# Pads of 448 and 64 bytes around the two weight tiles of one product

## The chip, the core and the metric

One core of a Trainium2 chip runs the whole program in one launch. The metric is device time in microseconds. The engines that matter are TensorE (PE; its weight loads are listed apart as PEld), VectorE (DVE), ScalarE (ACT), GpSimd (POOL) and the queue of SyncE (SP), which issues nearly all transfers.

## What is computed

Linear attention with random features, then a mixing of tokens by a low-rank matrix, then an MLP with a residual, all in float32:

```python
def phi(x):
    proj = np.einsum('bhsd,md->bhsm', x, omega)
    sq = np.sum(x * x, axis=-1, keepdims=True) / 2.0
    h = proj - sq
    h = h - np.max(h, axis=-1, keepdims=True)
    return np.exp(h) / np.sqrt(m)
kv = np.einsum('bhsm,bhsd->bhmd', k_p, v)
num = np.einsum('bhsm,bhmd->bhsd', q_p, kv)
den = np.einsum('bhsm,bhm->bhs', q_p, z)[..., None] + 1e-06
# x = num / den, heads joined: (8, 576, 512)
h = xt @ U @ V
u = x + h.transpose(0, 2, 1)
ch = np.maximum(u @ w_ch1, 0.0) @ w_ch2        # 512 -> 2048 -> 512
return (u + ch).astype(np.float32)
```

## The kernel before

The 8 x 576 = 4608 rows go through three phases. The first (to about 325 us) does the attention and the mixing; its projections, L766 to L768, multiply a feature matrix (`omh`, `oml`, the moving operand) with transposed queries and keys (`xh`, `xl`, the stationary operand). Each result u goes to DRAM.

The second phase is the MLP's first layer. Rows are taken in 9 chunks of 512, the 2048 hidden units in 4 groups of 512, and each product of a chunk with a group is done by Strassen's scheme: 7 products of halves, numbered 0 to 6. Every operand is split into a high and a low part of type float32r, so a product is 2 (f) x 2 (k) x 3 (high by high, low by high, high by low) = 12 matmuls of 128x128 by 256 columns (L1007). There the weight slice `wh` or `wl` is the stationary operand, and u (`uh`, `ul`) is the moving one. The results g go through the ReLU to DRAM.

The third phase is the second layer: 36 steps (chunk, half j, half s), again 7 products each, 12 matmuls a product (L1390). Here g (`gh`, `gl`) is stationary and the weights move. Step n has s = n mod 2, and k = 0 to 3 uses weight group (4 s + k) // 2, so that group 0 serves k = 0 and 1 of the 18 steps with s = 0.

Weights live in slots, one pair (`wh`, `wl`) for each group g and product i, got by `w_slot(g, i)`; a tile is 128 x 512 float32, 2048 bytes of each partition. Groups 0 and 1 lie in the pool `wa` at the bottom of the left stack, in the order in which they are first asked for; groups 2 and 3 lie in `wb` on the right stack. A slot serves the first layer, and later, by `w_place(g)`, the second layer's weights of the same group. Chunk 0 reads u from the pool `up` like the others, but chunk 1's u operands (`guest`) are put into slots of group 3 (`place=lambda i: w_slot(NG - 1, i + 2)`), and appear as `wh`, `wl` on both sides of L1007. Chunks 0 and 1 run first, in the order (0,0), (0,1), (1,0), (1,1), (0,2), (1,2) of (chunk, group); at group 3 their products alternate; after that come chunks 2 to 8, four groups each.

What lies where is set by stacks of pools and by pads: `shifted(stack, by)` opens a pool with one tile of `by` bytes that no instruction uses. Above `wa` on the left stack come `dec` (tiles of 2048 and 4096 bytes), then, in the first layer, a pad of 704 bytes and `up` (tiles of 2048 bytes, u among them). In the second layer `dec` and `up` are closed, and a pad of 320 bytes and the pool `vp` with the g operands stand straight above `wa`. So, modulo 512 bytes, u lies 704 and g 320 behind the weights. In the kernel as allocated every weight slot, left or right, begins 448 bytes past a multiple of 512.

All orders on the engines that touch the change are written out by hand (`K` keeps an instruction in program order).

Of the kernel before, what the change touches and what calls it, by code (L numbers as in the profile page):

```python
# [9 lines left out]
F32 = mybir.dt.float32  # L10
F32R = mybir.dt.float32r
# [18 lines left out]
def performer_mlp_kernel(ctx: ExitStack, tc, q, k, v, omega, U, V, w1, w2, out):  # L30
# [12 lines left out]
    P = 128  # L43
# [36 lines left out]
    wpools = {g: wa for g in range(EARLY_GROUPS)}  # L80
# [145 lines left out]

    def w_slot(g, i):
        i = (i - 2) % 7 if g == NG - 1 else i
        return [wpools[g].tile([P, 2, 2 * P], F32R, name=f"w{a}{g}_{i}") for a in "hl"]

    def operand(g, i):
        if (g, i) not in wops:
            if g == NG - 1 and i < 2:
                if not spares:
                    room = late["rx"].tile([P, 2, PIECE, 2], U32, name="graw0").bitcast(F32R)
                    spares.extend(room.rearrange("p s (k t) w -> p (s k) (t w)", k=2)[:, j] for j in range(4))
                wops[g, i] = [x.rearrange("p (k t) -> p k t", k=2) for x in spares[2 * i : 2 * i + 2]]
            else:
                wops[g, i] = w_slot(g, i)
        return wops[g, i]  # L240
# [826 lines left out]
    def w_place(g):  # L1067
        return lambda i: w_slot(g, i)
# [5 lines left out]
    tp = aside.enter_context(tc.tile_pool(name="tp", bufs=1))  # L1074
    guest_raws = loads(1, tp)
    guest = prepare(1, next(guest_raws), place=lambda i: w_slot(NG - 1, i + 2), lows=(VE, G_) * 3 + (VE,), pool=tp)
    for n, _ in enumerate(mixers[0]):
        if n == 2:
# [166 lines left out]
    for n in range(2, len(order)):  # L1245
        c, g = order[n]
# [123 lines left out]
    for n in range(NS):  # L1370
# [9 lines left out]
        for i in range(PRODUCTS):  # L1380
# [4 lines left out]
            for k in range(4):  # L1385
                g, f = divmod(now.s * 4 + k, 2)
# [70 lines left out]
```

## Time and profile before

| | us |
|---|---|
| median of 3 runs | 1037.36 |
| lowest and highest run | 1030.91, 1040.03 |
| the profiled execution | 1036.24 |
| its span | 1034.3 |
| TensorE busy | 1007.6 (97%) |
| VectorE busy | 850.4 (82%) |
| ScalarE busy | 613.7 (59%) |
| GpSimd busy | 519.8 (50%) |

The span is the time from the first to the last instruction of the profile. Matmuls are pipelined: a duration in the profile (276 ns, for example) is longer than the distance between the starts of two neighbours, and the next begins while the last is still under way. Where nothing waits, it is the distance between starts that adds up to the time.

### The profile page before, as it was taken

The page shows a single profiled execution, that of the slowest core. Times are in us where ns is not written, and L with a number is a line of the kernel's source. Part 1 is how long each engine was busy: PE and PEld are TensorE (multiplying, and loading weights), DVE is VectorE, ACT ScalarE, POOL GpSimd, SP SyncE. Part 2 cuts the span into 40 slices and gives each one's busy share as a digit, 9 for nine tenths or more (in the row PEclk, how much of TensorE's full clock was granted, in tenths as well). Part 3 has the DMA queues.
Part 4 walks back from the last instruction along what each step waited for, and adds up shares of the span by engine and source line. Part 5 has one row for each costly group of instructions (what it writes and reads, how often), then busy time and mean ns, then how long its engine had stood idle before and what let it go on. Part 6 is the DMA issues. An engine that isn't in the chain of part 4 may idle for free.

```text
span 1034.3 us, 23873 instructions
## 1 busy us (share of the span) xinstructions
PE 1007.6 (97%) x8497; PEld 985.9 (95%) x8497; DVE 850.4 (82%) x1502; ACT 613.7 (59%) x1483; POOL 519.8 (50%) x457
## 2 busy tenths in 40 slices
PE   8999899999998989999999999999999999999998
PEld 7899899999996989999999999999999999999998
DVE  4798898898898787766567465779999999999995
ACT  5889789989885555545355353764535444444442
POOL 3446766967534544233415214445664645646643
PEclk9899899999999999999999999999999999999999
DMA  7687578587444775987678678874545545455451
GB/s 138 137 167 147 114 176 171 107 184 154 87 103 96 210 183 137 248 246 196 186 202 215 187 183 255 254 234 135 211 147 177 181 166 175 150 184 174 142 175 51
DMA packets 380630, 175.51 MB, mean 170 GB/s; under 512 B 275680, under 2 KB 353504, under 8 KB 376032
## 3 DMA queue, kind: packets, MB, share of 16 engines
q1 hardware_dynamic: 378144, 173.70, 63.4%
q8 instruction: 67, 1.10, 0.4%
q10 hardware_dynamic: 2368, 0.30, 0.2%
q14 instruction: 51, 0.42, 0.1%
HBM read 109.97 MB, written 63.96 MB: 168 GB/s over the span
## 4 chain that ended last, share of the span: by engine, by line
PE 56%; DVE 3%; DMA 3%; issue 2%; ACT 1%; POOL 1%; SPq 0%; ACTq 0%; DVEq 0%; POOLq 0%
PE p_p L1390 9%; PE p_q L1390 8%; PE p_n L1390 7%; PE p_n L1007 7%; PE p_p L1007 5%; PE p_q L1007 5%; PE p_kv L1390 4%; PE p_kv L1007 4%; PE p_m L1007 4%; PE p_m L1390 2%; DVE g L995 1%; DMA g<-g 1%; DMA graw<-in_moe_w_ch_dram 1%; DMA graw<-g 0%; DVE wl L537 0%
## 5 line engine op out<-in xcount | busy, mean ns | idle before, releaser
L781 ACT ACTIVATE e<-p_p,nm 128x128 f32<-128x128 f32 x576 | 166.2, 397 | 27.9 <-DVE nm L774 22.3
L1228 ACT CAST gh<-gs 128x512 fp32r<-128x512 f32 x140 | 86.4, 622 | 153.4 <-DVE gs L1200 90.3
L1200 POOL TENSOR_TENSOR gs<-graw 128x512 f32<-128x512 f32 x70 | 111.2, 1600 | 122.7 <-DMA graw<-g 92.4
L991 ACT ACTIVATE g<-g 128x512 f32<-128x512 f32 x105 | 66.3, 633 | 158.0 <-DVE g L995 102.1
L647 POOL TENSOR_TENSOR xl<-xT,xh 128x384 fp32r<-128x384 f32 x96 | 97.4, 1030 | 100.2 <-ACT xh L643 82.0
L1235 DVE TENSOR_TENSOR gl<-gs,gh 128x512 fp32r<-128x512 f32 x140 | 136.5, 982 | 6.9 <-ACT gh L1228 6.0
L774 DVE TENSOR_REDUCE nm<-p_p 128x4 f32<-128x512 f32 x144 | 98.1, 682 | 27.6 <-PE p_p L768 12.5
L184 POOL TENSOR_TENSOR wf<-wf,low 128x512 int32<-128x512 int32 (+2 forms) x35 | 43.7, 1249 | 138.3 <-ACT g L991 81.1
L766 PE MATMUL p_p<-omh,xh 128*128 128x256 f32 x288 | 93.8, 326 | 3.9 <-ACT e L781 2.8
L1315 POOL TENSOR_TENSOR u<-u,p 128x256 f32<-128x256 f32 x72 | 80.3, 1144 | 27.4 <-DVE u L1315 24.9
L1235 DVE TENSOR_TENSOR gl<-graw,gh 128x512 fp32r<-128x512 f32 x107 | 83.1, 800 | 3.7 <-ACT gh L1228 3.7
L768 PE MATMUL p_p<-omh,xl 128*128 128x256 f32 x288 | 82.0, 285 | 0.6 <-POOL xl L647 0.6
L767 PE MATMUL p_p<-oml,xh 128*128 128x256 f32 x288 | 81.8, 284 | 0.0
L1390 PE MATMUL p_p<-wh,gh 128*128 128x256 f32 x288 | 79.5, 276 | 0.0
L1390 PE MATMUL p_p<-wl,gh 128*128 128x256 f32 x288 | 79.5, 276 | 0.0
L1390 PE MATMUL p_p<-wh,gl 128*128 128x256 f32 x288 | 79.5, 276 | 0.0
L1228 ACT CAST gh<-graw 128x512 fp32r<-128x512 f32 x107 | 63.6, 619 | 25.4 <-PE p_n L1390 4.8
L1390 PE MATMUL p_q<-wh,gl 128*128 128x256 f32 x276 | 76.5, 277 | 0.1
L1390 PE MATMUL p_q<-wh,gh 128*128 128x256 f32 x276 | 76.3, 276 | 0.0
L1390 PE MATMUL p_q<-wl,gh 128*128 128x256 f32 x276 | 76.3, 276 | 0.0
L724 PE MATMUL p_n<-kv,eT 128*128 128x65 f32 x512 | 72.6, 270 | 1.0 <-ACT eT L709 0.7
L1007 PE MATMUL p_n<-ul,wh 128*128 128x256 f32 x256 | 70.9, 277 | 1.2 <-POOL ul L537 1.2
(271 smaller groups left out, 3978.9 us busy)
## 6 DMA issues: line engine op xcount, KB each, us to landing
g<-g SPq DMA_DIRECT2D x282, 128.0 KB, 2.7
graw<-g SPq DMA_DIRECT2D x35, 1024.0 KB, 5.3
raw<-in_moe_w_ch_dram SPq DMA_DIRECT2D x23, 512.0 KB, 4.6
u_dram<-ut SPq DMA_DIRECT2D x36, 256.0 KB, 2.6
u<-u_dram SPq DMA_DIRECT2D x36, 256.0 KB, 2.6
out_dram<-u SPq DMA_DIRECT2D x36, 256.0 KB, 2.5
kt<-in_k_dram SPq DMA_DIRECT2D x120, 72.0 KB, 2.5
qt<-in_q_dram SPq DMA_DIRECT2D x120, 72.0 KB, 2.6
```

Of the source, the lines that this page charges most:

```text
L647: nc.gpsimd.tensor_tensor(out=self.xl[-1], in0=self.turned, in1=f32(self.xh[-1]), op=ALU.subtract)
L766: nc.tensor.matmul(o, part.xh[g][:, ts], oh, start=True, stop=False)
L767: nc.tensor.matmul(o, part.xh[g][:, ts], ol, start=False, stop=False)
L768: nc.tensor.matmul(o, part.xl[g][:, ts], oh, start=False, stop=True)
L774: nc.vector.tensor_reduce(out=self.nm[:, :n], in_=self.pp[:, :n], axis=AX.X, op=ALU.max, negate=True)
L781: nc.scalar.activation(out=self.e[:, j, :], in_=self.pp[:, j, :], func=AF.Exp, bias=self.nm[:, j : j + 1])
L1007: K(nc.tensor.matmul(p[:, f, :], x[:, k, fs], y[:, k, :], start=first, stop=(k == 1 and y is ul), skip_group_check=True,))
L1200: K(engine.tensor_tensor(out=to, in0=self.val[x], in1=self.val[y], op=op))
L1228: K(nc.scalar.copy(out=h, in_=v))
L1235: K(nc.vector.tensor_tensor(out=l, in0=v, in1=f32(h), op=ALU.subtract))
L1315: K(engine.tensor_tensor(out=out, in0=x, in1=y, op=ALU.add))
L1390: K(nc.tensor.matmul(acc[bank][:, half, :], x[:, ks], y[:, f, :], start=(now.s == 0 and k == 0 and half == 0 and x is h and y is wh), stop ...
```

## The change

`w_slot` asks for a pad of 112 floats (448 bytes) before the tiles of group 0, product 1, and for one of 16 floats (64 bytes) after them. Nothing else differs.

```diff
     def w_slot(g, i):
         i = (i - 2) % 7 if g == NG - 1 else i
-        return [wpools[g].tile([P, 2, 2 * P], F32R, name=f"w{a}{g}_{i}") for a in "hl"]
+        pool = wpools[g]
+        if (g, i) == (0, 1):
+            pool.tile([P, 112], F32, name="before")
+        tiles = [pool.tile([P, 2, 2 * P], F32R, name=f"w{a}{g}_{i}") for a in "hl"]
+        if (g, i) == (0, 1):
+            pool.tile([P, 16], F32, name="behind")
+        return tiles
```

## Rows read from the trace of the kernel before

**Rows 1.** The page, busy time of each engine, share of the span, instructions.

```profile
span 1034.3 us, 23873 instructions
PE 1007.6 (97%) x8497; PEld 985.9 (95%) x8497; DVE 850.4 (82%) x1502; ACT 613.7 (59%) x1483; POOL 519.8 (50%) x457
```

**Rows 2.** The page, chain that ended last, share of the span by engine and line.

```profile
PE 56%; DVE 3%; DMA 3%; issue 2%; ACT 1%; POOL 1%; SPq 0%; ACTq 0%; DVEq 0%; POOLq 0%
PE p_p L1390 9%; PE p_q L1390 8%; PE p_n L1390 7%; PE p_n L1007 7%; PE p_p L1007 5%; PE p_q L1007 5%; PE p_kv L1390 4%; PE p_kv L1007 4%; PE p_m L1007 4%; PE p_m L1390 2%; DVE g L995 1%; DMA g<-g 1%; DMA graw<-in_moe_w_ch_dram 1%; DMA graw<-g 0%; DVE wl L537 0%
```

**Rows 3.** Matmuls by stretch: us, PE busy (count under way), granted clock, DMA share, GB/s.

```profile
440.00:520.00 80.00, 80.00 (x708) 1.00 0.78 209
696.00:702.00 6.00, 6.00 (x54) 1.00 0.64 259
710.00:1010.00 300.00, 300.00 (x2650) 1.00 0.51 169
```

**Rows 4.** Groups of instructions, 386 to 394 us: count | busy, mean duration | idle before.

```profile
L1007 PE MATMUL p_n<-wh,wh 128*128 128x256 f32 x16 | 4.5, 283 | 0.0
```

**Rows 5.** Groups of instructions, 440 to 450 us.

```profile
L1007 PE MATMUL p_p<-uh,wh 128*128 128x256 f32 x12 | 3.3, 276 | 0.0
```

**Rows 6.** Groups of instructions, 720 to 730 us.

```profile
L1390 PE MATMUL p_q<-wh,gh 128*128 128x256 f32 x13 | 3.6, 276 | 0.0
```

**Rows 7.** Chain in order of time, first layer: start, us, what.

```profile
394.28 1.38 PE p_q L1007 x12
395.66 1.42 PE p_p L1007 x12
...
455.38 1.36 PE p_kv L1007 x12
```

**Rows 8.** Chain in order of time, near the end of the second layer.

```profile
1011.63 5.44 PE p_p L1390 x48
```

**Rows 9.** Groups of instructions, 696 to 702 us.

```profile
L1390 PE MATMUL p_q<-wh,gh 128*128 128x256 f32 x15 | 4.2, 281 | 0.0
```

**Rows 10.** Timeline of TensorE, 693 to 705 us: start, duration, line, operation.

```profile
693.73 0.28 PE L1390 MATMUL p_m<-wh,gh 128*128 128x256 f32 x1
...
694.91 0.28 PE L1390 MATMUL p_m<-wl,gh 128*128 128x256 f32 x1
...
695.26 0.28 PE L1390 MATMUL p_q<-wl,gh 128*128 128x256 f32 x1
695.62 0.38 PE L1390 MATMUL p_q<-wh,gl 128*128 128x256 f32 x1
...
702.67 0.28 PE L1390 MATMUL p_kv<-wl,gh 128*128 128x256 f32 x1
704.21 0.38 PE L1390 MATMUL p_kv<-wh,gl 128*128 128x256 f32 x1 [1.26 <-DVE gl L1235]
...
704.79 0.28 PE L1390 MATMUL p_kv<-wh,gh 128*128 128x256 f32 x1
704.90 0.28 PE L1390 MATMUL p_kv<-wl,gh 128*128 128x256 f32 x1
```

**Rows 11.** Groups of instructions, attention phase, 200 to 320 us.

```profile
L768 PE MATMUL p_p<-omh,xl 128*128 128x256 f32 x108 | 30.2, 280 | 0.0
L767 PE MATMUL p_p<-oml,xh 128*128 128x256 f32 x108 | 30.1, 279 | 0.0
```

**Rows 12.** Line L272, the casts into weight tiles: duration in ns, minimum/median/maximum.

```profile
L272 ACT CAST wh<-wf x38: 389/408/557, 92.4 to 409.9; 128x256 fp32r<-128x256 f32 x38
```

**Rows 13.** Timeline of TensorE, first 10 us.

```profile
9.44 0.41 PE L766 MATMUL p_p<-omh,xh 128*128 128x256 f32 x1
...
10.07 0.32 PE L766 MATMUL p_p<-omh,xh 128*128 128x256 f32 x1
```

## The prediction

> **What bounds the kernel now.** I read the page's busy times first: TensorE is busy for 97% of the span and its weight loads for 95%, while VectorE stands at 82% and the others at 59% and 50% [rows 1]. The chain that ended last says the same: 56% of it is matmuls, and its seven costliest lines are the products of L1390 and L1007, the second and the first layer of the MLP [rows 2]. Then I cut the span into stretches: TensorE has no idle time in any of those shown, and the granted clock is 1.00, the 2.4 GHz level [rows 3]. So in the two product phases the time is the number of matmuls times the distance between the starts of two neighbours, which I call the beat. Only what changes the beat, or stops TensorE, moves the end.
>
> The change moves tiles in memory and nothing else, so I looked for places where the same matmul (256 columns, 128x128 weights) has another beat. Three exist. From 710 to 1010 us there are 2650 matmuls in 300 us, 113 ns each [rows 3]; in the chain in order of time 48 of them take 5.44 us, 113.3 ns [rows 8]. Their mean duration is 276 ns in both phases [rows 5, 6]. Between 386 and 394 us the duration is 283 ns [rows 4]; twelve of this kind take 1.42 us in the chain, against 1.36 us for twelve ordinary ones [rows 7], so the beat there is 118 to 120 ns (7 ns more in the duration, 0.06/12 = 5 ns in the chain with its ends mixed in). Between 693 and 702 us the duration is 281 ns [rows 9], and ten beats from 693.73 to 694.91 us take 1.18 us, 118 ns [rows 10].
>
> What sets them apart is partly where the operands lie. While one matmul streams its moving operand, the next one's stationary operand is loaded, so I take the distance from the moving tile to the stationary tile, modulo 512 bytes. Every tile concerned is a multiple of 512 bytes, so the pads alone set it. In layer 1 the weights are stationary and u moves; u lies 704 bytes of pad behind the weights, hence distance -704, that is 320. In layer 2 the weights move and g is stationary, 320 bytes of pad behind them: again 320. Chunk 1 is the exception: its u operands live in the weight slots of group 3, which are allocated at the same residue as all weight slots, hence distance 0. These are the `wh,wh` rows, the slow ones at 283 ns [rows 4]. So distance 0 costs up to 7 ns a matmul and 320 costs none of that.
>
> **The change part by part.** The 448 bytes ahead move the two tiles of group 0, product 1; the 64 behind make the sum 512. All tiles behind them on the left stack, u and g included, move by 512 together; tiles on the right stack stay. A step of 512 is free by the rows: within one product the weight slices start 0, 512, 1024 and 1536 bytes into their tile, and the beat is 113.3 over whole products [rows 8]. The pads themselves are two tiles that no instruction touches: 0.
>
> The distances that change are those of one product in 28. (a) Layer 1: eight chunks run group 0, product 1 with u in its own pool, 12 matmuls each, 96 in all; distance 320 becomes 256. (b) Chunk 1's twelve go from 0 to 448. (c) Layer 2: the same slots hold the second layer's weights of group 0, used in the 18 steps with s = 0, in k = 0 and 1: six matmuls each, 108 in all; distance 320 becomes 384. That is 216 of the 6048 matmuls of the two layers (9 chunks x 28 products x 12, and 36 steps x 84).
>
> No row here has a dense 256-column stream at 256 or 384, so I bound them. From above by the worst beat seen, distance 0: 204 x 7 ns = 1.4 us. From below by an estimate: in the first 10 us, before the stream comes up to speed, matmuls of this shape start 0.21 us apart (three in 0.63) [rows 13]; a stream twice as fast with no loss at all would have 105 ns, 8 below 113.3, so -216 x 8 ns = -1.7 us. For the value I go by neighbours. Distance 256 has 320 for its neighbour and is the farthest there is from 0: I take 113.3, cost 0. Distance 384 lies between 320 and 448, and 448 is there in the attention phase, where omh moves while the next xh or xl is loaded, 64 bytes below it: 279 and 280 ns [rows 11]. Half of the 3 to 4 ns is 2 ns: 108 x 2 = 0.2 us. Chunk 1's twelve gain 12 x 3 ns, under 0.04 us: 0. Then the passage itself: when chunk 0 and chunk 1 alternate by product, the twelve at 320 that follow a product at 0 take 1.38 us instead of 1.36 [rows 7], 0.02 us for getting back. With 8 + 18 such passages that is 0.5 us. The sum is +0.7 us, all of it on TensorE, which has nothing to hide it.
>
> A rule speaks against any effect. The row first: neighbours that differ only in where the moving operand lies take 283 against 276 ns [rows 4, 5]. The Trainium skill (TensorE: Matmul & The Clock Gate, Step-by-step: what each phase is for) says that loading the next weights takes no SBUF read bandwidth from the running matmul, since TensorE has two independent read ports. By that rule the change costs 0 in place of 0.7 us; the trace does not agree with it at distance 0.
>
> Writes into the moved tiles are six: four in layer 1 (a cast and a subtraction per half) and two in layer 2. The casts run 389 to 557 ns already [rows 12]; even that whole spread six times is 1.0 us, on engines that are 59% and 50% busy [rows 1], hidden unless a product waits for them. No queue is passed and no DMA added. Buffers that reuse bytes of closed pools overlap the same predecessors as before, since left tiles move together and no boundary between left and right pools is crossed by the 512.
>
> **The rivals.** *The beat stays shifted (slower).* The 118 ns between 693 and 702 us are at distance 320, the same as the 113 ns later on, with no waiting between neighbours. A stop at 695.26 leaves it at 118; the stop from 702.67 to 704.21 ends with starts 113 ns apart [rows 10], and it stays so to the end [rows 8]. So the beat at 320 has two states, 118 and 113.3, and a disturbance decides which; the state then holds for as long as TensorE doesn't stop. A product at another distance is a disturbance that comes 9 times in layer 1 and 18 times in layer 2. If it leaves the stream at 118, layer 2 loses 35 steps x 84 x 4.5 ns = 13 us and layer 1, from chunk 2 on, 7 x 336 x 4.5 ns = 11 us: 1049 to 1051 us for one layer, 1062 for both. Against it: while chunks 0 and 1 alternate, the return from distance 0 ends in the 113 state within twelve matmuls (1.38 us, not 1.42) [rows 7], and so do the five like it; a seventh has a wait in it. It decides by what the first product behind the moved one shows: 276 or 281 ns. A milder form holds only until the next stop, say 800 matmuls, 3.6 us.
>
> *The distance frees the stream (faster).* If one of the distances let the loads pass unhindered and the state held behind it, the beat could fall towards that 105, 8 ns for 2900 matmuls in layer 2: 23 us less, 1014. Against it: in 2650 matmuls no stretch lies below 113 [rows 3].
>
> *The pads do nothing.* No instruction reads or writes them, so they might take no space; the time would be that of before, 1037. Against it: the pads of before are of the same kind. Were they dropped, u would lie at distance 0 like chunk 1's operands, and its rows would show 283 and not 276 ns [rows 4, 5].
>
> **How the numbers follow.** The profiled execution took 1036.24 us, 1034.3 of it the span; the median of the three runs is 1037.36, 1.1 more. 1036.24 + 0.7 + 1.1 = 1038.0. I give 0.77 to the forecast (with it the small cases: rule of no effect, either bound), 0.04 to the pads doing nothing, 0.15 to the shifted beat, of which 0.03 is the mild form, and 0.04 to the freed stream. The range is the spread of the runs, 1030.9 to 1040.0, with half of the lower bound's 1.7 us taken off (1030) and the mild shift's 3.6 us put on (1044); beyond lie the lock in a whole layer and the freed stream, under 2 in 10. One per cent, 10.4 us, is about what a measurement of this kernel can tell from no change. Slower by more needs the lock through a layer: 0.12. Faster by more needs the freed stream: 0.04. The rest, 0.84, is within it.
>
> **What would show it.** Right: the groups of L1007 and L1390 keep 276 ns; the twelve of group 0, product 1 take 1.36 to 1.44 us, and the six with g likewise a few hundredths more; the next product is back at 1.36 to 1.38; span within a few us of 1034. Wrong: 281 ns over long stretches behind a moved product (lock), under 276 (freed), or new idle time on TensorE before 414 us. Nothing at all at the moved products would mean that distances other than 0 are all alike, or that the pads took no space.

## The result

| | before | changed |
|---|---|---|
| median, 22 runs each | 1037.28 | 1039.51 |
| lowest and highest | 1027.07, 1055.47 | 1037.04, 1047.95 |
| span of the profiled execution | 1034.3 | 1041.8 |

The ratio of the changed kernel to the one before is 1.0067, with a 95% interval of 1.0044 to 1.0090: 7 us slower. That ratio leaves out the 6 of 22 runs of the kernel before that lie more than 1.5% above its fastest; over all runs the medians differ by 2.2 us only, and on the chip of the last experiments, where 15 of 30 are left out, the median of the kernel before is 1.2 us above that of the changed one. So a loss against all executions of before is not shown. What the change did is seen best in the spread: 10 of the 22 runs of before are faster than any of the changed kernel, and 4 are slower than all of them.

In both traces every engine runs the same instructions in the same order. The page of the changed kernel, busy time (to be held against [rows 1]):

```profile
span 1041.8 us, 23873 instructions
PE 1015.2 (97%) x8497; PEld 993.6 (95%) x8497; DVE 851.1 (82%) x1502; ACT 613.5 (59%) x1483; POOL 520.3 (50%) x457
```

TensorE took 7.6 us longer for the same 8497 matmuls; the busy time of no other engine changed by more than 0.7. Matmuls by stretch of the changed kernel (us, busy with the count under way, granted clock, DMA share, GB/s), one from each layer:

```profile
600.00:660.00 60.00, 60.00 (x512) 1.00 0.72 209
760.00:1000.00 240.00, 240.00 (x2115) 1.00 0.51 169
```

The same two stretches of the kernel before:

```profile
600.00:660.00 60.00, 60.00 (x532) 1.00 0.78 229
760.00:1000.00 240.00, 240.00 (x2120) 1.00 0.51 170
```

The loss lies in the first layer: there 20 matmuls fewer fit into 60 us, in the second 5 fewer into 240. (The line numbers of the changed kernel are 6 higher: L1013 is L1007, L1396 is L1390.) Groups of the changed kernel, the first at 640 to 650 us, the second at 900 to 910 us (count | busy, mean ns | idle before):

```profile
L1013 PE MATMUL p_p<-uh,wh 128*128 128x256 f32 x12 | 3.4, 281 | 0.0
...
L1396 PE MATMUL p_p<-wh,gh 128*128 128x256 f32 x16 | 4.4, 276 | 0.0
```

The first layer shows the 281 ns of [rows 9], where [rows 5] had 276. The chain of the changed kernel in order of time (start, us, what) shows how it comes to that. Chunk 2 starts with the row at 414.92; its first 24 matmuls are products 0 and 1 of group 0, the second of them the moved one:

```profile
414.92 2.82 PE p_q L1013 x24
417.73 1.41 PE p_kv L1013 x12
...
454.48 2.85 PE p_q L1013 x24
457.33 1.41 PE p_kv L1013 x12
...
738.20 2.77 PE p_kv L1396 x24
740.97 1.36 PE p_m L1396 x12
742.33 5.44 PE p_q L1396 x48
```

In the chain of the kernel before, a pair of products in the second layer that answers to the one at 738.20:

```profile
731.47 2.72 PE p_kv L1390 x24
```

Behind the moved product every ordinary twelve takes 1.41 us, 118 ns a matmul, and not the 1.36 of [rows 7]; it stays so over 324 matmuls up to the next moved product (457.33 to 495.5), and then again, to the end of the layer. In the second layer a pair of products with the moved one takes 2.77 us instead of 2.72, and the next twelve are back at 1.36. So the first moved product of these chunks, entered at 113 ns, throws the stream into the slower of its two beats; each later one in layer 1 is entered at 118 and leaves 118. In layer 2 none throws it there.

The account: in the seven chunks from 2 to 8, 2352 matmuls at 4.5 ns more (117.8 against 113.3) are 10.6 us; 18 passages of 0.05 us in layer 2 are another 0.9. The span grew by only 7.5 us. By the starts of the matmuls (some 0.17 us ahead of the chain's rows), the kernel before took 270.99 us from chunk 2 to the start of layer 2 (414.01 to 685.00), the changed one 277.17 (414.75 to 691.92), 6.2 more: 4.4 us of stops, and of slow beats behind them, in the kernel before have no counterpart in the changed one, where no matmul of this stretch waits for another engine. Most of the 4.4 lie in one stretch of the kernel before (columns as above):

```profile
526.00:580.00 54.00, 52.02 (x444) 0.97 0.81 217
```

The same stretch in the changed kernel:

```profile
526.00:580.00 54.00, 54.00 (x461) 1.00 0.82 223
```

Here the kernel before stood still for 1.98 us (until a wait for VectorE's `g`, L995, ended at 575.81), and from 576.90 on 15 matmuls ran some 213 ns apart at a granted clock of 0.50, the lower of the two levels, 1.2 GHz. The row of one such microsecond, and two of the 15 in the timeline of TensorE (start, us each, what):

```profile
577.00:578.00 1.00, 1.00 (x7) 0.50 0.04 11
...
577.11 0.41 PE L1007 MATMUL p_kv<-uh,wh 128*128 128x256 f32 x1
577.33 0.41 PE L1007 MATMUL p_kv<-uh,wl 128*128 128x256 f32 x1
```

The changed kernel, in its slower beat, had neither the stop nor the low clock and got through 17 matmuls more. How much of the loss is won back in this way differs between executions: a second profile of the kernel before (before_again) went from chunk 2 to layer 2 in 268.13 us, 9.0 less than the changed kernel.

### The profile page after: what moved, and what is told of

Same layout as the page of the kernel before. It is cut to its first block, busy times and chain, and to the rows that moved or that the text cites. A ratio compares the mean times of both kernels' runs of the same rounds, so it can differ in the third digit from the quotient of the medians.

```text
span 1041.8 us, 23873 instructions
## 1 busy us (share of the span) xinstructions
PE 1015.2 (97%) x8497; PEld 993.6 (95%) x8497; DVE 851.1 (82%) x1502; ACT 613.5 (59%) x1483; POOL 520.3 (50%) x457
## 4 chain that ended last, share of the span: by engine, by line
PE 60%; DVE 2%; issue 1%; ACT 1%; POOL 1%; DMA 0%; ACTq 0%; DVEq 0%; SPq 0%
PE p_p L1396 9%; PE p_q L1396 8%; PE p_n L1013 8%; PE p_n L1396 7%; PE p_p L1013 6%; PE p_q L1013 6%; PE p_kv L1396 4%; PE p_kv L1013 4%; PE p_m L1013 4%; PE p_m L1396 2%; DVE g L1001 1%; DMA graw<-g 0%; POOL wl L283 0%; DVE gl L1241 0%; ACT g L997 0%
## 5 line engine op out<-in xcount | busy, mean ns | idle before, releaser
L653 POOL TENSOR_TENSOR xl<-xT,xh 128x384 fp32r<-128x384 f32 x96 | 97.3, 1030 | 103.6 <-ACT xh L649 89.4
L1396 PE MATMUL p_p<-wh,gl 128*128 128x256 f32 x288 | 79.5, 276 | 0.0
L1396 PE MATMUL p_p<-wh,gh 128*128 128x256 f32 x288 | 79.5, 276 | 0.0
L1396 PE MATMUL p_p<-wl,gh 128*128 128x256 f32 x288 | 79.5, 276 | 0.0
L1396 PE MATMUL p_q<-wh,gl 128*128 128x256 f32 x276 | 76.3, 276 | 0.0
L1396 PE MATMUL p_q<-wh,gh 128*128 128x256 f32 x276 | 76.2, 276 | 0.0
L1396 PE MATMUL p_q<-wl,gh 128*128 128x256 f32 x276 | 76.2, 276 | 0.0
L730 PEld LDWEIGHTS p_n<-kv,eT 128*128 128x128 f32 x512 | 69.1, 196 | 4.3 <-ACT eT L715 1.7
```

Of the source, the lines that this page charges most:

```text
L653: nc.gpsimd.tensor_tensor(out=self.xl[-1], in0=self.turned, in1=f32(self.xh[-1]), op=ALU.subtract)
L730: nc.tensor.matmul(pn[:, h, :], eT[:, h, :], kv[:, h, s // 5, :], start=True, stop=True)
L1396: K(nc.tensor.matmul(acc[bank][:, half, :], x[:, ks], y[:, f, :], start=(now.s == 0 and k == 0 and half == 0 and x is h and y is wh), stop ...
```

## The experiments

All are variants of the pads; the computation is complete in each. L1 and L2 are the distances (moving to stationary, modulo 512) of the moved product in the two layers; the beats are worked out from the count of matmuls in 600 to 660 us and in 760 to 1000 us of each profile, of which the rows are shown where a verdict rests on them.

| run | L1 | L2 | matmuls in 60 us, L1 | in 240 us, L2 | median, us | ratio to before (95%) |
|---|---|---|---|---|---|---|
| changed | 256 | 384 | 512 | 2115 | 1039.51 | 1.0067 (1.0044 to 1.0090) |
| p512 | 320 | 320 | 512 | 2120 | 1033.5 | 1.0 (0.9955 to 1.0046) |
| p64 | 384 | 256 | 527 | 2116 | 1032.54 | 0.9999 (0.9963 to 1.0036) |
| p192 | 0 | 128 | 512 | 2115 | 1038.01 | 1.0066 (1.0037 to 1.0095) |
| p320 | 128 | 0 | 531 | 2116 | 1032.26 | 0.9979 (0.9942 to 1.0016) |
| reset | 0, then 128 | 128, 0 | 529 | 2110 | 1032.91 | 0.9984 (0.9950 to 1.0017) |
| p256 | 64 | 64 | 512 | 2120 | 1039.14 | 1.0042 (0.9995 to 1.0088) |
| g12 | 384, twice | 256, twelve | 530 | 2111 | 1031.55 | 0.9989 (0.9940 to 1.0037) |
| all192 | 448 everywhere | 448 everywhere | 511 | 2120 | 1049.45 | 1.0134 (1.0077 to 1.0192) |
| umove | 256, u moved | 320 | 528 | 2120 | 1034.23 | 1.0017 (0.9976 to 1.0059) |
| after_again | 256 | 384 | 512 | 2115 | 1040.53 | 1.0064 (1.0034 to 1.0094) |
| p320_again | 128 | 0 | 531 | 2115 | 1033.15 | 0.9984 (0.9956 to 1.0011) |
| before_again, one run | 320 | 320 | 532 | 2120 | 1029.48 | |

Theory: a product at distance 256 in layer 1 locks the stream into the 118 ns beat (*lock*). Rivals: that all tiles behind were shifted; or that a moved product costs by itself, whatever its distance.

### Other distances: p512, p64, p192, p320

Each has one of the four new lines in place of the pad ahead; the pad behind, not shown, is changed to match.

```diff
         if (g, i) == (0, 1):
-            pool.tile([P, 112], F32, name="before")    # 448 bytes
+            pool.tile([P, 128], F32, name="before")    # p512: 512, none behind
+            pool.tile([P, 16], F32, name="before")     # p64: 64, 448 behind
+            pool.tile([P, 48], F32, name="before")     # p192: 192, 320 behind
+            pool.tile([P, 80], F32, name="before")     # p320: 320, 192 behind
```

> Pads of 512 bytes ahead and none behind: everything behind moves as in the change, but no distance modulo 512 changes. Lock theory (a product at distance 256 puts the first layer into the 118 ns beat until the next stop): no stretch of 118 ns follows group 0, product 1; both beats occur, decided by stops, as before; ratio to before 1.00, within 0.5%. Rival (moving all tiles behind by 512 bytes is what costs): 118 ns all through the first layer as in the changed kernel, ratio 1.005 to 1.010.

The median lies 1.0 us under that of before. But its profiled execution (span 1041.3) was at 118 ns through most of layer 1. The timeline of TensorE tells why:

```profile
431.76 0.28 PE L1011 MATMUL p_n<-uh,wh 128*128 128x256 f32 x1
...
432.10 0.28 PE L1011 MATMUL p_n<-uh,wh 128*128 128x256 f32 x1
...
432.33 0.28 PE L1011 MATMUL p_n<-ul,wh 128*128 128x256 f32 x1
432.75 0.38 PE L1011 MATMUL p_n<-uh,wh 128*128 128x256 f32 x1
...
433.09 0.28 PE L1011 MATMUL p_n<-ul,wh 128*128 128x256 f32 x1
...
434.27 0.28 PE L1011 MATMUL p_q<-uh,wh 128*128 128x256 f32 x1
```

Before the stop at 432.33 three beats take 0.34 us, 113 ns; behind it ten take 1.18 us, 118 ns, and nothing brings the stream back until the layer ends. That is no moved product but an ordinary stop; product 1 of this chunk, ahead of it, had left 113. Shifting everything by 512 bytes is no cause by itself: the ratio is 1.0, and ten runs span 1025.86 to 1043.23 (31 of the kernel before on that chip: 1027.11 to 1056.95).

> Pads of 64 ahead and 448 behind: the distances of the change swapped, 384 in the first layer and 256 in the second. Lock theory: the first layer falls back to 113 ns behind each moved product (276 ns durations), and the second layer runs at 118 ns (281 ns) all through: plus 12 to 13 us there, minus up to 10 in the first layer against the changed kernel; about 1045 us. Rival (the first layer alone is sensitive, whatever the distance): the first layer at 118 ns, the second at 113, about 1040.

The first half came true, the second fell. Layer 1 at distance 384 returns to 113 ns: chain of p64,

```profile
490.05 2.78 PE p_q L1013 x24
492.83 1.36 PE p_kv L1013 x12
```

and once, at 608 us, such a product took the stream out of the 118 ns beat into which a stop had put it. But layer 2, with distance 256, stayed at 113 (2116 matmuls in 240 us). So 256 does not lock as such.

> Pads of 192 ahead and 320 behind: distance 0 in the first layer, 128 in the second. Lock theory: distance 0 has been seen to leave 113 ns (chunks 0 and 1 alternating), so the first layer stays at 113 ns behind every moved product, its twelve take 1.42 to 1.44 us; 128 was not seen, either state. If it leaves 113 too, about 1032 us; if 118, about 1045. Rival (any other distance than 320 leaves 118): both layers at 118, about 1053.

Here the theory failed the other way. Distance 0, which had seemed harmless while chunks 0 and 1 alternated, locks layer 1 just as 256 does. Chain of p192:

```profile
487.44 2.85 PE p_q L1013 x24
490.30 1.41 PE p_kv L1013 x12
```

These are the 2.85 and 1.41 of the changed kernel to the digit, and the ratio is the same too.

> Pads of 320 ahead and 192 behind: distance 128 in the first layer, 0 in the second. Lock theory: the second layer stays at 113 ns, the six matmuls at distance 0 cost 7 ns each; the first layer is decided by 128, not seen so far: about 1032 us if it leaves 113, about 1041 if 118. Rival (any other distance than 320 leaves 118): both layers at 118, about 1053.

Distance 128 leaves 113 ns, and layer 2 at distance 0 does as well. Four distances and two classes: 0 and 256 lock layer 1, 128 and 384 free it. That looks like a period of 256 bytes, half of what I had taken.

### The period: p256

Here and in the next two, w_slot takes the bytes ahead and behind from a table:

```diff
+        ahead, behind = {(0, 1): (256, 256)}.get((g, i), (0, 0))
```

> Pads of 256 ahead and 256 behind: 64 in both layers, where 320 was. If the period is 256 bytes, the moved product's matmuls keep 276 ns and nothing is disturbed: no passage to be seen, twelve in 1.36 us, both beats by luck of the stops, ratio to before 1.00. If the period is 512, as the prediction took it, 64 is a new distance: the twelve show other durations than their neighbours.

The moved product can't be seen. Chain of p256, where the first 24 are products 0 and 1; first in the beat of 113 (here only 21 of the 24, cut at 489.91), then after a stop in that of 118:

```profile
489.91 2.38 PE p_q L1014 x21
492.29 1.36 PE p_kv L1014 x12
...
607.11 2.83 PE p_q L1014 x24
609.93 1.41 PE p_kv L1014 x12
```

21 at 113.3 are 2.38 us, 24 at 117.8 are 2.83. Distance 64 behaves as 320 and leaves either beat as it was. With 0 like 256, and 128 like 384, the period is 256. The ratio of 1.0042 goes with an interval that holds 1: the runs (1027.86 to 1048.51) spread like those of before.

### Undoing the lock by a second disturbance: reset

```diff
+        ahead, behind = {(0, 1): (192, 128), (0, 2): (0, 192)}.get((g, i), (0, 0))
```

> The slow version with one more disturbance behind it: product 1 of group 0 at distance 0 in the first layer, as with pads of 192 and 320, and product 2 right behind it at distance 128 (second layer: 128 and 0). Lock theory, with a period of 256 bytes: product 1 puts the stream into the 118 ns beat and product 2 takes it out, so the first layer runs at 113 ns from product 3 on; about 5 to 8 us less than with product 1 alone (1038), ratio to before 0.995 to 1.00. Rival (each moved product costs by itself, more of them cost more): the first layer at 118 ns as before, ratio 1.007 or above.

Chain of reset: products 0 and 1, then 2, 3, 4 and on.

```profile
487.38 2.80 PE p_q L1014 x24
490.18 1.42 PE p_kv L1014 x12
491.60 1.37 PE p_m L1014 x12
492.98 1.36 PE p_q L1014 x12
```

Product 1 runs at 120 ns as in p192 (2.80 less 1.36 for product 0), product 2 at distance 128 takes 1.42, and from product 3 on all is at 113. Two moved products are 5 us faster than one of them alone (medians of 1032.91 and 1038.01, on two chips; ratios to before of 0.9984 and 1.0066). The rival that each costs by itself is out.

### Which operand is displaced: g12 and umove

Layer 2 hadn't locked at 0 or 256. There only six matmuls of the product are moved, and it is the moving operand that is displaced, where in layer 1 it is the stationary one.

```diff
+        ahead, behind = {(0, 1): (64, 192), (1, 1): (64, 192)}.get((g, i), (0, 0))     # g12
```

> Product 1 of groups 0 and 1 both moved by 64 bytes (sums 256 each): distance 384, like 128, in the first layer, 256, like 0, in the second, and there in all twelve matmuls of a product instead of six. If twelve at distance 0 modulo 256 are what locks the slow beat in, the second layer now runs at 118 ns: plus 13 us there, about 1045; the first layer stays at 113. If the second layer can't be locked at all: the passages cost some 0.1 us each, 1033.

Layer 2 with all twelve at 256 ran on at 113 (2111 in 240 us, nine fewer than before, for the longer passages), and layer 1 at distance 384 at 113 as well:

```profile
600.00:660.00 60.00, 60.00 (x530) 1.00 0.76 228
```

The number of moved matmuls was not it.

```diff
     def u_operand(i):
-        return [late["up"].tile([P, 2, HT], F32R, name=n, bufs=UB) for n in ("uh", "ul")]
+        up = late["up"]
+        if i == 1:
+            up.tile([P, 16], F32, name="before")
+        tiles = [up.tile([P, 2, HT], F32R, name=f"{n}{i}", bufs=1) for n in ("uh", "ul")]
+        if i == 1:
+            up.tile([P, 48], F32, name="behind")
+        return tiles
```

> The weights stay; the u tiles of product 1, the moving operand, go up by 64 bytes (sum 256), so that product 1 of every group has distance 256 in the first layer, four times a chunk. If any twelve matmuls at distance 0 modulo 256 lock the first layer, it runs at 118 ns from chunk 2 on, about 1040 to 1044. If it matters which operand moves (chunks 0 and 1 alternating, and the second layer, where the moving operand is the displaced one, went back to 113): the first layer runs at 113 ns behind each such product, each passage costs some 0.08 us, 28 of them 2 us, about 1035.

Chain of umove:

```profile
487.60 2.78 PE p_q L1013 x24
490.38 1.38 PE p_kv L1013 x12
491.76 1.36 PE p_m L1013 x12
```

Layer 1, distance 256, twelve matmuls, as in the change; only u was displaced in place of the weights. The product costs its 0.06 us, the next one 0.02, and the stream is back. Of 28 such products in chunks 2 to 8, 27 were entered at 113 ns and left 113 behind them; the one that was entered at 118, after a stop, left 113 as well. So the distance of the product alone doesn't decide: between neighbours at 320, a step of the stationary operand to 256 and back leaves 118, and the same step of the moving operand leaves 113. Why the two differ, no run shows; the next experiment shows that it isn't the operand alone either.

### A distance for all: all192

```diff
-    shifted(phase, 704)
+    shifted(phase, 576)
...
-                    shifted(ctx, 320)
+                    shifted(ctx, 448)
```

> No pads around weights; the pads under u and g are changed (704 to 576, 320 to 448), so that every product of chunks 0 and 2 to 8 has distance 448 (192 modulo 256) in both layers. Where chunk 1's twelve had 448 they ran at 113 ns, eleven of twelve. If 192 has no slow state: 276 ns all through both layers but for chunk 1, also behind stops, runs within 5 us of each other, about 1030. If it has one like 320: both beats, spread as before, 1035.

192 modulo 256 has the slow beat too: the profiled execution (span 1040.5) ran through layer 1 at 118 and nearly all of layer 2 at 113. Its three other runs lie at 1049 to 1050; no profile shows where those 7 us went.

What put layer 1 at 118 stands in its chain, where chunks 0 and 1 alternate by product (the twelve of chunk 0 at 448 first, those of chunk 1 at 0 second):

```profile
397.97 1.42 PE p_q L1007 x12
399.38 1.45 PE p_p L1007 x12
...
418.06 1.41 PE p_kv L1007 x12
```

In the kernel before, the twelve at 320 that follow a product at 0 were back at 113 (1.38, [rows 7]); here the twelve at 448 are at 118 (1.42), and chunk 2 goes on so. The weights are the same for both chunks, so both are steps of the moving operand. At the start of layer 2 it is the other way round. There the first three products take g, the stationary operand, from another pool and run at 120 ns, as at distance 0; the timelines of TensorE show ten beats of the fourth, of all192 (from 696.48) and of the changed kernel (from 696.23):

```profile
696.48 0.28 PE L1390 MATMUL p_q<-wh,gh 128*128 128x256 f32 x1
697.61 0.28 PE L1390 MATMUL p_q<-wl,gh 128*128 128x256 f32 x1
...
696.23 0.28 PE L1396 MATMUL p_q<-wh,gh 128*128 128x256 f32 x1
697.40 0.28 PE L1396 MATMUL p_q<-wl,gh 128*128 128x256 f32 x1
```

Ten beats take 1.13 us at 448 and 1.17 at 320. Coming back from products at 120 ns, the stream ends at 118 after a step of the moving operand at 448 or of the stationary one at 320, and at 113 in the two other cases. For 448 that rests on this one profile.

### Once more: after_again, p320_again, before_again

> The changed kernel once more, on the same chip: first layer at 118 ns in every execution, 1037 to 1048, ratio to before 1.005 to 1.008, and 7 us above the pads of 320 and 192.

Runs of 1036.21 to 1043.81, the lock again in each of chunks 2 to 8 of its profile; its median lies 7.4 us above that of the next, over all runs of both and on one chip.

Its layer 2 shows a thing that the account of the changed kernel leaves out. Chain of after_again, early in layer 2:

```profile
709.24 5.65 PE p_p L1396 x48
714.89 4.19 PE p_n L1396 x36
719.09 5.44 PE p_p L1396 x48
```

The first 48 run at 118, the last 48 at 113, and the second of the three products between them is the moved one, at 384: it took the stream out of the slow beat, and in p192, at 128, one did the same. In the first step of layer 2 the moved product, entered at 118 in four profiles (changed, after_again, p192, reset), left 118. So the change may also cut slow stretches of layer 2 short. That would fit the slowest executions of before, which the changed kernel lacks, but no profile of before with a slow layer 2 was taken, and it is not shown.

> Pads of 320 and 192 once more, with more rounds: distance 128 in the first layer, which took the stream out of the 118 ns beat. If that is so in every execution, no run lies above 1038, the median is 2 to 4 us under that of before, the ratio of the comparison 0.997 to 0.999 (it leaves out the slowest runs of before).

Twelve runs, 1029.38 to 1036.4, median 1033.15; the 30 runs of before on that chip reach from 1026.95 to 1058.98, median 1041.7. No run lies above 1038, as expected, and the median is 8.5 us under that of before, not 2 to 4. The ratio is 0.9984 (0.9956 to 1.0011), no gain that can be told. Its chain shows a chunk of layer 1 that a stop had put at 118, and the moved product (in the 24 from 489.77) that ends it:

```profile
486.95 2.83 PE p_n L1013 x24
489.77 2.84 PE p_q L1013 x24
...
493.99 1.36 PE p_m L1013 x12
```

All runs together say the same of layer 1. Of the 44 of the changed kernel, after_again and p192 (stationary operand at 0 or 256) none is under 1036.2; of the 32 of p64, p320 and p320_again (at 128 or 384) none is over 1037.4.

> One more profile of the kernel before. If which beat the first layer takes is decided by its stops, this execution has other stretches of 118 ns than the first, and its time goes with them: 4.5 ns for each matmul in such a stretch, 1028 without any, up to 1050 with all of a layer.

1029.48 us. Matmuls by stretch of this execution:

```profile
600.00:660.00 60.00, 60.00 (x532) 1.00 0.77 230
```

This one was at 113 ns through nearly all of layer 1 from chunk 2 on, as the first profile of before. That both of these were, while p512 and p256, with the same distances modulo 256, were caught at 118 from some stop on, is what the spread of before would look like if it is drawn at each stop; no profile of before itself with a locked layer was taken.

## Why the prediction was wrong, by its own steps

**What bounds it** held: TensorE's beat sets the time in both layers, and nothing else changed. The pads took their space, and the shift of the rest by 512 was free, as argued (p512).

**The term for getting back is the step that failed.** The sum gave 0.02 us for the return behind each moved product, as if the stream always came back to 113 ns. In layer 1 it didn't: behind the first moved product of chunk 2 it stayed at 118 to the end of the layer, 10.6 us of beat, of which 6.2 were left as time between the two profiles.

**The distances were worked out modulo 512.** That is the smaller error. The rows had 0, 320 and 448, and none of these can tell 512 from 256. I took 256 for "the farthest there is from 0" and gave it the price 0; it is 0 itself. The twelve cost 1.44 us instead of 1.36, which is the upper bound that I had set from the rows at distance 0 (7 ns each) and then not taken: some 0.6 us in all. Knowing the period would not have given the rest, since by [rows 7] the stream comes back from distance 0. For 384 I took half of what separates 320 from 448 and 0.02 us for the way back, 0.03 us a passage; it measured 0.05 (2.77 for 2.72), so layer 2 was right in place and 0.4 us too small in size. The row it came from was no price of 448: in all192 the products at 448 run at either beat.

**The rival "the beat stays shifted" is what happened**, in layer 1 alone: where I looked for it (the first product behind the moved one, 281 ns), and at about the gross price that I had put on it, 11 us against 10.6 measured. I gave it 0.15. What spoke against it, the returns to 113 while chunks 0 and 1 alternate, was read off passages in which the moving operand is displaced. In layer 1 the change displaces the stationary one, and umove against the changed kernel shows that at a distance of 320 around the product this difference decides. The row was good; it answered another question. The second mistake in it was the net price: between the two profiles layer 1 from chunk 2 on cost 6.2 us and not 11, since at 113 the stream stood still at times (526 to 580 us) and at 118, in the changed kernel, it didn't; against before_again it cost 9.0.

**The rule of no effect** does not hold here. The Trainium skill (TensorE: Matmul & The Clock Gate, Step-by-step: what each phase is for) says that loading the next weights steals no read bandwidth from the running matmul; the same instructions in the same order ran at beats of 113, 118 and 120 ns here, by the addresses and by what had gone before. Whether the two reads hinder each other, no run shows.

**The time** itself, 1039.5, lay inside the range of 1030 to 1044 and within the 1% to which I had given 0.84. That is luck: it started from 1037.36, the middle of three runs of a kernel whose runs spread over 28 us, and another three would have set another base. The forecast was a cost of 0.7 us, and the 7 of the ratio are ten times that, with an interval that keeps clear of it.

## What to carry to other kernels

Where a dense stream of matmuls sets the time, take the distance between starts, not the duration or the busy share, and look for stretches of equal matmuls with different beats: two values with no waiting in between meant here that the stream has states, and then a disturbance of a dozen matmuls can cost a whole layer. When a row from elsewhere is used as evidence that a disturbance heals, check that it displaces the same operand. Placing one product so that it frees the stream (here 128 bytes modulo 256 for the stationary operand, between neighbours at 320) bounds how long a bad beat can last, which shows in the spread before it shows in the best time.

## What the runs showed of the hardware

For this shape, 256 columns of float32r at a granted clock of 1.00, a weight load and a matmul that run side by side settle into beats of 113.3, 118 or 120 ns by the distance of their operands modulo 256 bytes; 320, 64 and 448 have both 113 and 118. A beat of either kind lasts unchanged over hundreds of matmuls without a stop (324 at 118 in the changed kernel, some 2870 at 113 in layer 2 of the kernel before). A stop can flip it either way (to 118 at 432.33 in p512, to 113 at 702.67 in [rows 10]). Between products at 320, twelve matmuls of layer 1 with the stationary operand displaced to 0 or 256 leave 118, entered at 113 (changed, after_again, p192); displaced to 128 or 384 they leave 113, entered at either beat (p64, p320_again). With the moving operand displaced to 256 they left 113, 28 times of 28 (umove), while between products at 448 a moving operand displaced to 0 left 118 (all192). What the two beats are inside the engine is open.
